# Seven score tiles a pair of heads, of 128 queries, in place of eight of 112, in an attention and feed-forward kernel

## The chip, the cores and the metric

The kernel runs on one core of a Trainium2 chip. The metric is the device time of one execution in microseconds (us). Before the change three runs give a median of 1433.79 us (1432.87 to 1435.07).

## What is computed

Attention over 8 batches and 12 heads, 448 tokens, head size 64, with normed queries and keys, followed by a feed-forward block on 3584 tokens of 768:

```python
q_n, k_n = rmsnorm(q, g_q), rmsnorm(k, g_k)
scores = scale * q_n @ k_n.T
scores = scores - max(scores)            # over the keys, for each query
attn = exp(scores) / (sum + 1e-9)
x = attn @ v                             # heads side by side: 3584 x 768
h = relu(x @ w_in)                       # 768 x 2048
out = (s * h * h + b) @ w_out            # 2048 x 768
```

The change concerns the maximum over the keys alone. It is subtracted before the exponential, and divides out again in `attn`, so it has to be near the true maximum and need not equal it to the last bit.

## The kernel before

**Pairs and slots.** Two heads of a batch make a pair: 48 pairs, 6 for each batch. A pair has 8 slots (`W`), and the outer loop (`for s_ in range(FIRST, NSLOT + LAST + 2)`) walks over 384 slots, with 22 ahead of them and some behind. The order of every engine's instructions, the DMA queue SP among them, is the order in which the program issues them; nothing is reordered by a scheduler. `jobs[s]` is a table of what else each slot issues, filled by `at(slot, function, ...)`; within a slot the jobs stand in the order of the pairs and, for a pair, of the `at` calls. With s0 = 8p the first slot of pair p, the places that matter are:

- s0 - 19 and s0 - 15: `load_kq` and `spread` (DMA in: keys and queries, and the inverse norms, for head 0 and head 1); four slots later `scale` (GpSimd L362, VectorE L363), two more and `split_kq` (ScalarE casts into `ka` and `qa`, L381 and L382, then GpSimd L384 and L385). The first 9 pairs go through `load_rows`, `norm_rows`, `turn` and `split_turned` in place of these (L255 to L291).
- s0 - 10 and s0 - 6: `double_kb`, a DMA of the keys' high parts from `ka` into `kb` (L388 by way of `move`).
- s0 - 10 to s0 - 3: `score` (L400) and `maximum` (L411), one of each in a slot; a slot s works on unit s + 10 (`AHEAD`).
- s0 - 6 and s0 - 2: `shift`, a DMA that writes the negative maxima of a head as row 64 of `qb` (L388 too).
- s0 to s0 + 7: `score_t`, the transposed scores of 128 keys in two matmuls (L438, then L441, which reads row 64 of `qb`), `exponent`, and two slots later `weigh` (L497), the product with the values.

**Scores, twice.** The kernel multiplies queries and keys twice. The transposed product goes on to the exponential. The other (`score`) serves the maxima alone: with queries on the partitions, VectorE can reduce over the 448 keys. Its weights are 112 queries, every fourth one of a head (`"k (p c) -> k c p"`, c of 4); its moving operand is the head's 448 keys; four such tiles for a head, eight for a pair. `maximum` reduces each to one column of `nmx` (112 by 8). The partitions 0 to 63 of `ka` hold the keys' high parts and 64 to 127 the low parts, and both halves of `qa` the queries' high parts.

**Filler.** While batch b's attention runs, TensorE also does the first feed-forward product of batch b - 1 (`ffn_in`, L208): six matmuls in each slot from slot 56 on (`FILL`), 288 a batch. The feed-forward weights are converted from 64-bit words on the way (L133 to L151 for `w_in`, up to slot 90; L156 to L172 for `w_out`). Behind the slots come a short stretch without attention and then the second product (L814).

Of the kernel before, what the change touches and what calls it, by code (L numbers as in the profile page):

```python
# [9 lines left out]
F32 = mybir.dt.float32  # L10
F32R = mybir.dt.float32r
I32 = mybir.dt.int32
AF = mybir.ActivationFunctionType
ALU = mybir.AluOpType
AX = mybir.AxisListType
# [24 lines left out]
STEPS = {0: 4, 1: 5, 5: 6, 6: 7, 9: 8, 10: 9, 12: 10, 13: 11}  # L40

LATE = 12

OUT = (92, *range(110, 141, 6), *(48 * b + i for b in range(3, 8) for i in range(14, 43, 7)))

# [2 lines left out]
def attention_then_relu2_ffn(  # L48
# [30 lines left out]
    V, S, G, T = nc.vector, nc.scalar, nc.gpsimd, nc.tensor  # L79

    NPAIR, P, _, SEQ = kq.shape
# [4 lines left out]
    D = P // 2  # L86
    NP = NPAIR // B
    H = 2 * NP
    TILES = 2 * SEQ // P
    NV = 2 * NP  # L90
    NR = rows0.shape[0]
    NQ = 4
    QC = SEQ // NQ
# [8 lines left out]
    W = 8  # L102
# [137 lines left out]
    lp = last.enter_context(tc.tile_pool(name="lpool", bufs=1, side="right"))  # L240
    ap = early.enter_context(tc.tile_pool(name="apool", bufs=1))
    if True:
        raws, kqs, invs, vrs, nmxs, shs, tks = ({} for _ in range(7))
        sts, movers, avs, uzs, zts, zbs, us = ({} for _ in range(7))

        def load(p):
            raw = raws[p] = ap.tile([P, 2, TILES, D], F32, tag="raw", name=f"raw{p}")
            nc.sync.dma_start(raw, kq_rows[p])
# [8 lines left out]
        def norm_rows(p, j):  # L257
            raw = raws[p, j].rearrange("p t c d -> p (t c) d")
            n = 2 * NQ
            sq = lp.tile([QC, n, D], F32, tag="al", bufs=2, name=f"sq{p}_{j}")  # L260
            S.activation(
                sq.rearrange("p i d -> p (i d)"), raw.rearrange("p i d -> p (i d)"), AF.Square
            )
            yield
            ssq = ap.tile([QC, n], F32, tag="ssq", bufs=2, name=f"ssq{p}_{j}")
            V.tensor_reduce(out=ssq, in_=sq, op=ALU.add, axis=AX.X)
            yield
            ri = ap.tile([QC, n], F32, tag="ri", bufs=2, name=f"ri{p}_{j}")
            G.tensor_scalar(ri, ssq, 1.0 / D, 1e-6, ALU.mult, ALU.add)
            G.tensor_tensor(ri, ri, mhalf[:QC, :n], ALU.pow)  # L270
            G.tensor_tensor(raw, raw, ri.unsqueeze(2).broadcast_to([QC, n, D]), ALU.mult)
# [40 lines left out]
        def load_v(p):  # L312
            if p < NV:
                to = vrs[p] = ap.tile([P, NKC, 3, D], F32, tag=f"vs{p % 2}", name=f"vf{p}")
# [18 lines left out]
        def norm(p):  # L333

            raw = raws.pop(p).rearrange("p t c d -> p (t c) d")
            n = 2 * TILES
            S.activation(
# [10 lines left out]
        def keep(p):  # L348
            nc.sync.dma_start(
                i_d[p].rearrange("t (p c) -> p t c", c=TILES),  # L350
                invs.pop(p).rearrange("p (t c) -> p t c", c=TILES),
            )
# [14 lines left out]
        ka = [ap.tile([P, 2 * SEQ], F32R, name=f"ka{n}") for n in range(2)]  # L367
        qa = [ap.tile([P, 2 * SEQ], F32R, name=f"qa{n}") for n in range(2)]
        kb = [ap.tile([P, 2 * SEQ], F32R, name=f"kb{n}") for n in range(2)]
        qb = [ap.tile([P, 2 * SEQ], F32R, name=f"qb{n}") for n in range(2)]  # L370
        for t in qb:
            G.memset(t[D:P].bitcast(F32), 0.0)
        for t in kb:
            G.memset(t[D:P].bitcast(F32), 0.0)
            G.memset(t[D : D + 1].bitcast(F32), 1.0)

        def split_kq(p, j):

            t, n = kqs.pop((p, j)), p % 2
            a = slice(j * SEQ, (j + 1) * SEQ)  # L380
            S.copy(ka[n][:, a], t[:, 0])  # L381
            S.copy(qa[n][:, a], t[:, 1])  # L382
            yield
            G.tensor_tensor(ka[n][D:, a], t[D:, 0], ka[n][D:, a].bitcast(F32), ALU.subtract)  # L384
            G.tensor_tensor(qb[n][:D, a], t[:D, 1], qa[n][:D, a].bitcast(F32), ALU.subtract)  # L385

        def move(to, of):
            nc.sync.dma_start(to.bitcast(F32), of.bitcast(F32))  # L388
# [5 lines left out]
        def score(i):  # L394

            p, c = divmod(i, W)
            j, c = divmod(c, NQ)
            sh, bank = psum(f"sh{i}")
            a = slice(j * SEQ, (j + 1) * SEQ)
            T.matmul(  # L400
                sh[:QC, :SEQ], qa[p % 2][:, a].rearrange("k (p c) -> k c p", c=NQ)[:, c],
                ka[p % 2][:, a], start=True, stop=True,
            )
            shs[i] = sh, bank

        def maximum(i):
            p, c = divmod(i, W)
            if c == 0:
                nmxs[p] = ap.tile([QC, W], F32R, tag="nmx", bufs=2, name=f"nmx{p}")
            sh, bank = shs.pop(i)  # L410
            V.tensor_reduce(  # L411
                out=nmxs[p][:, c : c + 1], in_=sh[:QC, :SEQ], op=ALU.max, axis=AX.X, negate=True
            )
            free.append(bank)

        def shift(p, part):

            to = qb[p % 2][D : D + 1, part * SEQ : (part + 1) * SEQ]
            move(
                to.rearrange("o (p c) -> o p c", c=NQ), nmxs[p][:, part * NQ : (part + 1) * NQ]  # L420
            )
            if part:
                nmxs.pop(p)

        def chunk(i):
            p, g = divmod(i, W)
            j, kc = divmod(g, NKC)
            return p, j, kc, P if kc < 3 or p < NV else REST

# [17 lines left out]
        def exponent(i):  # L447
            p, j, kc, rows = chunk(i)
            st, bank = sts[i]
            if p < NV:  # L450
                e = lp.tile([P, SEQ], F32, tag="ah", bufs=3, name=f"e{i}")
# [7 lines left out]
        def split_e(i):  # L459
            p, j, kc, rows = chunk(i)  # L460
            if p < NV:
                return
# [4 lines left out]
        def split_e_lo(i):  # L467
            p, j, kc, rows = chunk(i)
            if p < NV:
                return  # L470
# [10 lines left out]
        def weigh(i):  # L481
# [6 lines left out]
            moved = movers.pop(i)  # L488
            if p < NV:
                of = vrs[p].rearrange("p c u d -> p c (u d)")  # L490
# [11 lines left out]
        def take(p, j):  # L502
# [5 lines left out]
            if j == 0:  # L508
                zts[p] = lp.tile([P, TILES], F32, tag="zt", bufs=2, name=f"zt{p}")

        def gather(p, j):
            zt, uz = zts[p], uzs[p, j]
            row = (1 - j) * D
            nc.sync.dma_start(
                zt[j * D : (j + 1) * D], uz[row : row + 1].rearrange("o (p c) -> o p c", c=TILES)
            )
# [6 lines left out]
        def divide(p, step):  # L523

            if step == 1:
                nc.sync.dma_start(z_d[p].rearrange("j (p c) -> (j p) c", c=TILES), zts.pop(p))
            elif step == 2:
                zb = zbs[p] = lp.tile([P, SEQ], F32, tag="zb", name=f"zb{p}")
                for j in range(2):
                    nc.sync.dma_start(  # L530
                        zb[j * D : (j + 1) * D], z_d[p][j : j + 1].broadcast_to([D, SEQ])
                    )
            else:
                zb = zbs.pop(p)
                u = us[p] = lp.tile([P, SEQ], F32, tag="u", bufs=NP, name=f"u{p}")
                for j in range(2):
                    a = slice(j * D, (j + 1) * D)
                    G.tensor_tensor(u[a], uzs.pop((p, j))[a], zb[a], ALU.mult)  # L538
# [96 lines left out]
        def at(s_, f, *a):  # L635
            jobs[s_].append((f, a))

        for p in range(NPAIR):
            s0 = W * p
            if p >= NR:  # L640
                at(s0 - 32, load, p)
                at(s0 - 28, norm, p)
                at(s0 - 24, keep, p)
            for j in range(2):
                s1 = s0 + 4 * j
                if p >= NR:
                    at(s1 - 19, load_kq, p, j)
                    at(s1 - 19, spread, p, j)
                    at(s1 - 15, scale, p, j)
                    at(s1 - 13, split_kq, p, j)  # L650
                else:
                    at(max(s1 - 28, FIRST), load_rows, p, j)
                    at(s1 - 20, norm_rows, p, j)
                    at(s1 - 13, turn, p, j)
                    at(s1 - 12, split_turned, p, j)
                at(s1 - 10, double_kb, p, j)
                at(s1 - 6, shift, p, j)
                at(s1 + 6, take, p, j)
                at(s1 + 7, gather, p, j)
            at(s0 - (9 if p >= NV else 5), load_v, p)  # L660
            if p >= NV:
                at(s0 - 3, split_v, p)
            at(s0 + 13, invert, p)
            at(s0 + 14, divide, p, 1)
            at(s0 + 16, divide, p, 2)
            at(s0 + 18, divide, p, 3)
# [82 lines left out]
        def t_step(k):  # L749
# [3 lines left out]
            if k + 1 < KS:  # L753
                t_sums(k + 1, G if k + 1 < LATE + 2 else V)

# [122 lines left out]
        with tc.manual_schedule(engines=ORDERED):  # L878
            begun = []
            for s_ in range(FIRST, NSLOT + LAST + 2):  # L880
# [5 lines left out]
                if s_ >= NSLOT + 2:  # L886
                    k, of = divmod(s_ - NSLOT - 5, 3)
# [77 lines left out]
            for x in range(ROUNDS):  # L965
                if LATE <= LATE + x < KS:
                    t_step(LATE + x)
                g_load(x + 5)
                g_sums(x + 3)
                g_split(x + 2)  # L970
                p, m = divmod(x, NM)
# [53 lines left out]
```

## Time and profile before

| | |
|---|---|
| median of three runs | 1433.79 us |
| the profiled execution | 1435.51 us, with a span of 1433.0 us and a mean granted TensorE clock of 0.99 |
| TensorE busy | 1394.2 us, 97% of the span |
| VectorE, ScalarE, GpSimd busy | 73%, 60%, 72% |
| score matmuls for maxima (L400) | 384 |
| maxima (L411) | 384, 618 ns each, 236.5 us of VectorE |
| DMA | 237.94 MB, 55.8% of the 16 engines' time |

In the profile PE is TensorE's matmul row and PEld its weight loads, DVE is VectorE, ACT is ScalarE, POOL is GpSimd, and SPq is the queue that issues DMAs. A group of instructions is listed by line, engine, tile written and tiles read, shapes and count; behind the bar stand its busy time, the mean of one in ns, and the idle time of the engine ahead of it with what ended it. The chain of waits follows the last instruction back, at each step to what released it. Matmuls overlap in the record: one that shows 367 ns is followed by the next after about 204 ns.

### The profile page before, as it was taken

How to read it: one execution, taken by the hardware profiler on the slowest of the kernel's cores; microseconds unless marked ns; L12 is line 12 of the kernel's file. 1: busy time of each engine (PE TensorE's matmuls, PEld its weight loads, DVE VectorE, ACT ScalarE, POOL GpSimd, SP SyncE). 2: the span in 40 equal slices, each digit the busy share in tenths (PEclk: the TensorE clock that was granted, in tenths of full speed). 3: DMA queues.
4: the chain of work that ended last, by engine and by line, in shares of the span. 5: the costliest groups of instructions: out<-in, count | busy, mean ns of one | idle time of the engine just before them, and what ended most of it. 6: DMA issues, size and time to landing. Idle time of an engine off the chain costs nothing.

```text
span 1433.0 us, 22188 instructions
## 1 busy us (share of the span) xinstructions
PE 1394.2 (97%) x6996; PEld 1268.3 (89%) x6996; DVE 1048.4 (73%) x1594; ACT 867.0 (60%) x1649; POOL 1031.6 (72%) x941
## 2 busy tenths in 40 slices
PE   7988999999999999999999999989899999999999
PEld 5666778899899899999989989969799999999998
DVE  6998987888888788788788787463666666666665
ACT  4777555777767776777677777543445444444443
POOL 7778888877777777777778776273686776667764
PEclk8999999999999999999999999989999999999999
DMA  4456777777677677677777766243333333333331
GB/s 131 133 153 167 223 230 219 214 225 222 203 235 220 200 233 222 186 235 230 203 211 234 214 179 201 90 140 119 104 104 89 118 96 96 96 102 108 95 95 66
DMA packets 209252, 237.94 MB, mean 166 GB/s; under 512 B 72848, under 2 KB 187024, under 8 KB 209136
## 3 DMA queue, kind: packets, MB, share of 16 engines
q1 hardware_dynamic: 209136, 236.54, 55.8%
q8 instruction: 55, 0.90, 0.3%
q14 instruction: 61, 0.50, 0.1%
HBM read 178.00 MB, written 47.11 MB: 157 GB/s over the span
## 4 chain that ended last, share of the span: by engine, by line
PE 84%; DVE 7%; DMA 3%; POOL 2%; issue 2%; ACT 2%; SPq 0%; DVEq 0%; ACTq 0%; POOLq 0%
PE ph L208 29%; PE m L814 27%; PE av L497 13%; PE sh L400 5%; PE st L438 5%; PE st L441 5%; DMA w64i<-in_dram 1%; DVE nmx L411 1%; DVE wai L140 1%; DVE wai L137 1%; DVE wai L142 1%; POOL u L538 1%; PE tk L278 1%; DVE t L742 1%; DVE wai L145 0%
## 5 line engine op out<-in xcount | busy, mean ns | idle before, releaser
L208 PE MATMUL ph<-x,wih 128*128 128x448 f32 x1536 | 494.6, 368 | 7.1 <-ACT x L545 3.8
L814 PE MATMUL m<-t,gh 128*128 128x384 f32 x1568 | 400.8, 336 | 3.3 <-ACT gh L795 2.6
L208 PEld LDWEIGHTS ph<-x,wih 128*128 128x128 f32 x1536 | 289.8, 189 | 40.7 <-issue 7.8
L208 PE MATMUL ph<-x,wil 128*128 128x448 f32 x768 | 297.1, 387 | 0.0
L411 DVE TENSOR_REDUCE nmx<-sh 112x1 fp32r<-112x448 f32 x384 | 236.5, 618 | 78.1 <-PE sh L400 75.9
L814 PEld LDWEIGHTS m<-t,gh 128*128 128x128 f32 x1568 | 284.0, 188 | 5.4 <-ACT gh L795 3.3
L814 PE MATMUL m<-t,gl 128*128 128x384 f32 x784 | 263.6, 336 | 2.1 <-DVE gl L796 2.1
L457 ACT ACTIVATE st<-st 128x448 f32<-128x448 f32 (+1 forms) x288 | 151.3, 525 | 186.8 <-PE st L441 183.8
L796 DVE TENSOR_TENSOR gl<-g,gh 128x896 fp32r<-128x896 f32 x112 | 130.0, 1161 | 145.4 <-ACT gh L795 141.4
L795 ACT CAST gh<-g 128x896 fp32r<-128x896 f32 x112 | 105.8, 945 | 215.4 <-POOL g L785 157.2
L781 POOL TENSOR_TENSOR g<-g 128x256 f32<-128x256 f32 x112 | 97.2, 868 | 133.0 <-DVE g L780 133.0
L497 PE MATMUL av<-ah,vs 128*128 128x448 f32 x576 | 165.0, 367 | 0.8 <-DVE al L478 0.5
L400 PE MATMUL sh<-ka,qa 128*112 128x448 f32 x384 | 148.3, 388 | 16.5 <-DVE ka L290 8.4
L208 PEld LDWEIGHTS ph<-x,wil 128*128 128x128 f32 x768 | 144.9, 189 | 19.3 <-issue 7.9
L438 PE MATMUL st<-qa,ka 128*128 128x448 f32 (+1 forms) x384 | 158.1, 412 | 2.4 <-ACT e L453 1.7
L465 ACT CAST ah<-st 128x448 fp32r<-128x448 f32 (+1 forms) x288 | 153.6, 533 | 1.3
L814 PEld LDWEIGHTS m<-t,gl 128*128 128x128 f32 x784 | 147.6, 188 | 3.4 <-DVE gl L796 3.4
L538 POOL TENSOR_TENSOR u<-uz,zb 64x448 f32<-64x448 f32 x96 | 133.2, 1387 | 20.3 <-DMA zb<-z_d 16.1
L478 DVE TENSOR_TENSOR al<-st,ah 128x448 fp32r<-128x448 f32 x216 | 132.7, 614 | 18.7 <-ACT ah L465 15.8
L441 PE MATMUL st<-qb,kb 128*128 128x448 f32 (+1 forms) x384 | 140.6, 366 | 0.0
L384 POOL TENSOR_TENSOR ka<-kq,ka 64x448 fp32r<-64x448 f32 x78 | 97.5, 1250 | 52.2 <-ACT ka L381 48.9
L400 PEld LDWEIGHTS sh<-ka,qa 128*112 128x112 f32 x384 | 107.5, 281 | 30.0 <-ACT wih L148 5.4
(85 smaller groups left out, 2432.6 us busy)
## 6 DMA issues: line engine op xcount, KB each, us to landing
kq<-in_dram SPq DMA_DIRECT2D x78, 448.0 KB, 5.0
rb<-i_d SPq DMA_DIRECT2D x78, 448.0 KB, 5.8
r_d<-r SPq DMA_DIRECT2D x128, 224.0 KB, 3.1
raw<-in_dram SPq DMA_DIRECT2D x39, 448.0 KB, 5.0
raw<-r_d SPq DMA_DIRECT2D x64, 256.0 KB, 2.8
w64i<-in_dram SPq DMA_DIRECT2D x24, 512.0 KB, 4.7
w64o<-in_dram SPq DMA_DIRECT2D x32, 384.0 KB, 5.1
kb<-ka SPq DMA_DIRECT2D x96, 112.0 KB, 3.6
```

What stands on the lines that cost most here:

```text
L208: T.matmul(ph[:, :SEQ], w[:, cc, f0 : f0 + P], xs[b, cc][:, part, :], start=n == 0, stop=n == 3 * NCC - 1,)
L400: T.matmul(sh[:QC, :SEQ], qa[p % 2][:, a].rearrange("k (p c) -> k c p", c=NQ)[:, c], ka[p % 2][:, a], start=True, stop=True,)
L411: V.tensor_reduce(out=nmxs[p][:, c : c + 1], in_=sh[:QC, :SEQ], op=ALU.max, axis=AX.X, negate=True)
L438: T.matmul(st[:rows, :SEQ], ka[n][:, keys], qa[n][:, q], start=True, stop=False)
L441: T.matmul(st[:rows, :SEQ], kb[n][:, keys], qb[n][:, q], start=False, stop=True,)
L457: S.activation(st[:rows, :SEQ], st[:rows, :SEQ], AF.Exp)
L465: S.copy(ah[:rows], sts[i][0][:rows, :SEQ])
L478: V.tensor_tensor(al, st[:rows, :SEQ], ah[:rows].bitcast(F32), ALU.subtract)
L497: T.matmul(av[:, :SEQ], x, a, start=kc == 0 and m == 0, stop=kc == 3 and m == len(todo) - 1,)
L538: G.tensor_tensor(u[a], uzs.pop((p, j))[a], zb[a], ALU.mult)
L796: V.tensor_tensor(gl, g9[:, 1:8], gh.bitcast(F32), ALU.subtract)
L814: T.matmul(to, g[:, sa], w, start=m == 0 and n == 0, stop=m == NM - 1 and n == 2,)
```

## The change

Each head's first 384 queries go through three score tiles of 128 queries (every third one). The last 64 queries of both heads share one tile. For it two tiles are new: `both_k`, with the high parts of head 0's keys on partitions 0 to 63 and of head 1's on 64 to 127, filled by two DMAs a pair (`stack_k`); and `both_q`, zero but for two 64 by 64 blocks on the diagonal, filled by two ScalarE copies a pair (`stack_q`). So this tile's scores leave out the keys' low parts. The slot table `UNITS` keeps units 0, 1, 2 for head 0, 4, 5, 7 for head 1 and 6 for the shared tile; the fourth slot of each eight has no score and no maximum. The maxima of the shared tile are moved into `qb` by two more DMAs (`shift_rest`).

The space is made by two moves: the squares of `norm_rows` (`sq`) go from a tag with two buffers to the tag `vr` with one, and the results `u` have five buffers and not six, with the last pair's in a buffer of `al`.

```diff
+UNITS = {0: (0, 0), 1: (0, 1), 2: (0, 2), 4: (1, 0), 5: (1, 1), 6: (2, 0), 7: (1, 2)}
...
+    NF = SEQ // P
+    FULL = NF * P
...
-            sq = lp.tile([QC, n, D], F32, tag="al", bufs=2, name=f"sq{p}_{j}")
+            sq = ap.tile([QC, n, D], F32, tag="vr", name=f"sq{p}_{j}")
...
+        both_k = ap.tile([P, SEQ], F32R, name="both_k")
+        both_q = ap.tile([P, P], F32R, name="both_q")
+        G.memset(both_q.bitcast(F32), 0.0)
+
+        def stack_k(p, j):
+            move(both_k[j * D : (j + 1) * D], ka[p % 2][:D, j * SEQ : (j + 1) * SEQ])
+
+        def stack_q(p):
+            for j in range(2):
+                a = slice(j * D, (j + 1) * D)
+                S.copy(both_q[a, a], qa[p % 2][a, j * SEQ + FULL : (j + 1) * SEQ])
...
-            j, c = divmod(c, NQ)
+            if c not in UNITS:
+                return
+            j, c = UNITS[c]
             sh, bank = psum(f"sh{i}")
-            T.matmul(
-                sh[:QC, :SEQ], qa[p % 2][:, a].rearrange("k (p c) -> k c p", c=NQ)[:, c],
-                ka[p % 2][:, a], start=True, stop=True,
-            )
+            if j < 2:
+                T.matmul(
+                    sh[:, :SEQ],
+                    qa[p % 2][:, a][:, :FULL].rearrange("k (p c) -> k c p", c=NF)[:, c],
+                    ka[p % 2][:, a], start=True, stop=True,
+                )
+            else:
+                T.matmul(sh[:, :SEQ], both_q, both_k, start=True, stop=True)
...
-                out=nmxs[p][:, c : c + 1], in_=sh[:QC, :SEQ], op=ALU.max, axis=AX.X, negate=True
+                out=nmxs[p][:, u : u + 1], in_=sh[:, :SEQ], op=ALU.max, axis=AX.X, negate=True
...
+        def shift_rest(p, part):
+            to = qb[p % 2][D : D + 1, part * SEQ + FULL : (part + 1) * SEQ]
+            move(to.rearrange("o (p c) -> o p c", c=1), nmxs[p][part * D : (part + 1) * D, 2 * NF :])
...
+                of = dict(tag="al", bufs=2) if p == NPAIR - 1 else dict(tag="u", bufs=NP - 1)
...
+            at(s0 - 10, stack_k, p, 0)
+            at(s0 - 7, stack_k, p, 1)
+            at(s0 - 7, stack_q, p)
+            for j in range(2):
+                at(s0 - 3, shift_rest, p, j)
```

More of the change, by code (lines that the diff above doesn't have):

```diff
@@ L396, in score @@
             p, c = divmod(i, W)
-            j, c = divmod(c, NQ)
+            if c not in UNITS:
+                return
+            j, c = UNITS[c]
             sh, bank = psum(f"sh{i}")
-            a = slice(j * SEQ, (j + 1) * SEQ)
-            T.matmul(
-                sh[:QC, :SEQ], qa[p % 2][:, a].rearrange("k (p c) -> k c p", c=NQ)[:, c],
-                ka[p % 2][:, a], start=True, stop=True,
-            )
+            if j < 2:
+                a = slice(j * SEQ, (j + 1) * SEQ)
+                T.matmul(
[5 more added lines that the diff above has]
+                T.matmul(sh[:, :SEQ], both_q, both_k, start=True, stop=True)
             shs[i] = sh, bank
@@ L408, in maximum @@
             if c == 0:
-                nmxs[p] = ap.tile([QC, W], F32R, tag="nmx", bufs=2, name=f"nmx{p}")
+                nmxs[p] = ap.tile([P, 2 * NF + 1], F32R, tag="nmx", bufs=2, name=f"nmx{p}")
+            if c not in UNITS:
+                return
+            j, c = UNITS[c]
             sh, bank = shs.pop(i)
+            u = j * NF + c
             V.tensor_reduce(
-                out=nmxs[p][:, c : c + 1], in_=sh[:QC, :SEQ], op=ALU.max, axis=AX.X, negate=True
+                out=nmxs[p][:, u : u + 1], in_=sh[:, :SEQ], op=ALU.max, axis=AX.X, negate=True
             )
@@ L416, in shift @@
         def shift(p, part):
-            to = qb[p % 2][D : D + 1, part * SEQ : (part + 1) * SEQ]
+            nmx, row = nmxs[p], qb[p % 2][D : D + 1, part * SEQ : (part + 1) * SEQ]
             move(
-                to.rearrange("o (p c) -> o p c", c=NQ), nmxs[p][:, part * NQ : (part + 1) * NQ]
-            )
-            if part:
-                nmxs.pop(p)
+                row[:, :FULL].rearrange("o (p c) -> o p c", c=NF),
+                nmx[:, part * NF : (part + 1) * NF],
+            )
+        def shift_rest(p, part):
+            to = qb[p % 2][D : D + 1, part * SEQ + FULL : (part + 1) * SEQ]
+            move(to.rearrange("o (p c) -> o p c", c=1), nmxs[p][part * D : (part + 1) * D, 2 * NF :])
         def chunk(i):
@@ L534, in divide @@
                 zb = zbs.pop(p)
-                u = us[p] = lp.tile([P, SEQ], F32, tag="u", bufs=NP, name=f"u{p}")
+                of = dict(tag="al", bufs=2) if p == NPAIR - 1 else dict(tag="u", bufs=NP - 1)
+                u = us[p] = lp.tile([P, SEQ], F32, name=f"u{p}", **of)
                 for j in range(2):
```

## The prediction

> **What bounds the kernel now.** I read the page first, for the engines and the chain of waits.
>
> ```profile
> PE 1394.2 (97%) x6996; PEld 1268.3 (89%) x6996; DVE 1048.4 (73%) x1594; ACT 867.0 (60%) x1649; POOL 1031.6 (72%) x941
> PE 84%; DVE 7%; DMA 3%; POOL 2%; issue 2%; ACT 2%; SPq 0%; DVEq 0%; ACTq 0%; POOLq 0%
> PE ph L208 29%; PE m L814 27%; PE av L497 13%; PE sh L400 5%; PE st L438 5%; PE st L441 5%; DMA w64i<-in_dram 1%; DVE nmx L411 1%; DVE wai L140 1%; DVE wai L137 1%; DVE wai L142 1%; POOL u L538 1%; PE tk L278 1%; DVE t L742 1%; DVE wai L145 0%
> ```
>
> TensorE carries 84% of the chain, and the score matmul itself (L400) 5%; the maximum (L411) only 1%. An average over stages hides where that is so. The busy times by stretch come next (PE, PEld, DVE, ACT, POOL, clock, DMA share, GB/s):
>
> ```profile
> 40.00:60.00 20.00, 17.59 (x76) 12.28 (x74) 18.49 (x30) 14.69 (x30) 12.96 (x13) 1.00 0.41 113
> 100.00:120.00 20.00, 17.72 (x73) 11.88 (x71) 18.62 (x32) 16.53 (x32) 17.59 (x16) 1.00 0.51 142
> 140.00:180.00 40.00, 38.89 (x163) 30.67 (x162) 37.10 (x47) 22.60 (x44) 35.62 (x28) 1.00 0.75 231
> 262.00:377.00 115.00, 115.00 (x564) 105.24 (x564) 94.96 (x156) 83.22 (x173) 89.67 (x67) 1.00 0.74 222
> ```
>
> There are two regimes. From 262 us on TensorE is never idle, 115.00 of 115 us, and 564 matmuls share that time: 204 ns each. That is one batch of 48 slots exactly (48 times 2 transposed scores, 1 score and 6 of filler, and 132 products with the values). Here a matmul less is time less. Early, no engine is full: VectorE leads with 18.5 of 20 us, TensorE follows with 17.6, and the chain passes between them. So I take the chain of waits by stage, in four windows (0 to 30, 30 to 130, 130 to 240, 240 to 900 us):
>
> ```profile
> by line: DMA w64i<-in_dram 21.4%; PE tk L278 10.0%; DVE nmx L411 7.6%; DVE wai L137 7.4%; PE sh L400 7.2%; issue 5.5%; DVE wai L145 4.7%; DVE wai L140 4.7%; DVE wai L142 4.3%; ACT wih L148 4.2%; ACT qa L287 3.5%; ACT ka L286 3.1%; SPq L255
> ...
> by line: PE av L497 13.2%; issue 10.0%; PE sh L400 7.3%; DVE nmx L411 5.9%; PE tk L278 5.4%; DMA raw<-in_dram 5.0%; DVE wai L140 4.8%; PE st L438 4.2%; POOL ri L270 3.9%; DVE wai L142 3.8%; PE st L441 3.7%; ACT qa L288 3.4%; DVE ka L290 3.1
> ...
> by line: PE ph L208 16.1%; DMA w64i<-in_dram 11.7%; PE av L497 10.6%; issue 7.0%; DVE wai L140 6.5%; DVE wai L137 6.3%; DVE nmx L411 5.3%; DMA zt<-uz 5.1%; DVE wai L142 4.9%; POOL u L538 4.5%; DVE ssq L342 3.7%; PE sh L400 3.6%; DVE kq L363
> ...
> by line: PE ph L208 49.7%; PE av L497 23.6%; PE st L438 8.4%; PE st L441 8.4%; PE sh L400 8.3%; DMA zb<-z_d 0.4%; DVE kq L363 0.2%; DVE ssq L342 0.2%; issue 0.1%; DVE ah L478 0.1%; DVE nmx L411 0.1%; ACT qa L382 0.1%; ACT st L457 0.1%; DVE
> ```
>
> In the last window the score is 8.3% of the chain and the maximum 0.1%; before 240 us both stand on it at 4 to 8%.
>
> **What is taken away.** One score and one maximum of eight go, in each of 48 pairs. I price them as an eighth of what the two hold of the chain, since a path that stays is a floor for the new time:
>
> - 0 to 30 us: (7.6 + 7.2)% of 30, by 8: 0.6 us.
> - 30 to 130: (5.9 + 7.3)% of 100, by 8: 1.6 us.
> - 130 to 240: (5.3 + 3.6)% of 110, by 8: 1.2 us.
> - 240 to 900: (0.1 + 8.3)% of 660, by 8: 6.9 us.
>
> That is 10.3 us. The last term agrees with a count: at 115 us for six pairs 660 us hold 34 of them, times 204 ns, 7.0 us. The other three are soft. If VectorE were the only bound, each of the first 8 pairs would give a whole maximum, and so would the 4 after them. The groups, with shapes kept apart:
>
> ```profile
> L411 DVE TENSOR_REDUCE nmx<-sh 112x1 fp32r<-112x448 f32 x384 | 236.5, 618 | 78.1 <-PE sh L400 75.9
> L400 PEld LDWEIGHTS sh<-ka,qa 128*112 128x112 f32 x384 | 107.5, 281 | 30.0 <-ACT wih L148 5.4 <-ACT qa L288 3.6 <-ACT e L453 3.3
> L441 PEld LDWEIGHTS st<-qb,kb 128*128 128x128 f32 x312 | 59.1, 190 | 12.9 <-issue 8.7
> L381 ACT CAST ka<-kq 128x448 fp32r<-128x448 f32 x78 | 43.2, 554 | 0.0
> L739 ACT CAST t<-w 128x192 fp32r<-128x192 f32 x16 | 5.6, 349 | 0.6 <-POOL w L731 0.4
> ```
>
> 12 times 0.618 (the first row) is 7.4 us in place of 3.4, so the upper end is 14.3 us. If those stages give nothing, because GpSimd (17.6 of 20 us at 100) or the DMAs hold them, it is 6.9 us.
>
> **The wider tile.** The reduction and the matmul run over the same 448 columns; 128 partitions for 112 add nothing to either. What widens is the weight load. Its row shows 281 ns for 112 strided columns, against 190 for 128 that lie together: longer than the 204 ns step. Does it show? The timeline in the full stage (start, duration):
>
> ```profile
> 402.72 0.37 PE L208 MATMUL ph<-x,wih 128*128 128x448 f32 x1
> ...
> 402.92 0.36 PE L208 MATMUL ph<-x,wil 128*128 128x448 f32 x1
> 402.93 0.28 PEld L400 LDWEIGHTS sh<-ka,qa 128*112 128x112 f32 x1
> 403.13 0.37 PE L400 MATMUL sh<-ka,qa 128*112 128x448 f32 x1
> ...
> 403.33 0.57 PE L208 MATMUL ph<-x,wih 128*128 128x448 f32 x2
> ```
>
> The starts are 0.20, 0.21 and 0.20 apart: the load of 281 ns costs 0.01 us at most. By columns it grows to 281 times 128/112, 321 ns. I take zero, and keep 40 ns for 6 of 7 units (288 in all, 11.5 us) as the other end, in a rival. The Trainium skill (TensorE: Matmul & The Clock Gate, Back-to-back issue gap) says that weight load and matmul together set the spacing in a stream of pairs, and its section on LDWEIGHTS that a load goes with the number of columns, at 1.2 a ns. By that rule 16 columns more would be 13 ns a unit, 3.8 us for 288 and a sum of some 5 us in place of mine; the trace does not follow the figure, since 112 columns take longer than 128 here, and the step does not show the load.
>
> **What is added.** Two ScalarE copies of 64 columns a pair. The two CAST rows differ by 256 columns and 205 ns, so 64 columns come to about 0.25 us (an estimate; 0.20 to 0.35 as bounds): 0.5 us a pair. In the full stage ScalarE is at 83 of 115 us and six pairs add 3.0; it stays under TensorE, and slot s0 - 7, where the copies stand, has no score to serve. Early, a quarter of 8 times 0.5 is my guess of what reaches the chain: 1.0 us, between 0 and 4.
>
> Four DMAs a pair: two like `kb<-ka` and two like `qb<-nmx`, from the DMA view of 262 to 377 us (KB each, median us from issue to landing):
>
> ```profile
> q1 hardware_dynamic: 19933, 25.40, 74.0%
> ...
> rb<-i_d SPq DMA_DIRECT2D x12, 448.0 KB, 5.8
> ...
> kb<-ka SPq DMA_DIRECT2D x12, 112.0 KB, 4.0
> ...
> qb<-nmx SPq DMA_DIRECT2D x12, 1.8 KB, 4.4
> ```
>
> 25.40 MB for six pairs is 4.2 MB a pair; 0.23 MB more is 5%, and takes the share from 0.74 to 0.78. Nothing waits for bandwidth there. At 130 to 240 us the chain does hold DMAs (11.7 and 5.1% of 110, 18.5 us); 5% of that is 0.9 us, between 0 and 2.
>
> **The new waits.** `shift_rest` at s0 - 3 waits on SP for the shared tile's maximum, issued a slot before; behind it on SP are the next-but-one pair's keys and norms, and the one who waits for it is L441 in slot s0, three slots on. Pair 20, with s0 at 392.7 us:
>
> ```profile
> 384.01 0.37 PE L400 MATMUL sh<-ka,qa 128*112 128x448 f32 x1
> 385.09 0.60 SPq L298 DMA_DIRECT2D kq<-in_dram  x1
> 385.74 0.59 SPq L358 DMA_DIRECT2D rb<-i_d  x1
> 385.80 0.62 DVE L411 TENSOR_REDUCE nmx<-sh 112x1 fp32r<-112x448 f32 x1
> ...
> 392.95 0.37 PE L441 MATMUL st<-qb,kb 128*128 128x448 f32 x1
> ...
> 395.02 1.57 DVE L363 SCALAR_TENSOR_TENSOR kq<-kq,gqk,rb 128x448 f32<-128x448 f32 x1
> ```
>
> The maximum ends at 386.42. With the 4.4 us of `qb<-nmx` the rest lands at 390.8 and L441 starts at 392.95: 2.1 us spare. The loads behind it move from 385.09 to about 387.7 (two issues of some 0.6 us), so `rb` is issued near 388.3 and lands at 394.1 by its 5.8 us; L363 reads it at 395.02: 0.9 us spare. Both waits cost nothing, and both margins are thin. The early slots are shorter, and there the same two margins are, for pair 1 (the shared unit's maximum and the L441 that needs it; the keys that `stack_k` moves and the shared score):
>
> ```profile
> 29.36 0.51 ACT L286 CAST ka<-tk 64x448 fp32r<-64x448 f32 x1
> ...
> 34.89 0.37 PE L400 MATMUL sh<-ka,qa 128*112 128x448 f32 x1
> ...
> 36.27 0.62 DVE L411 TENSOR_REDUCE nmx<-sh 112x1 fp32r<-112x448 f32 x1
> ...
> 41.48 0.37 PE L441 MATMUL st<-qb,kb 128*128 128x448 f32 x1
> ```
>
> 36.89 + 4.4 is 41.3, just ahead of 41.48; 29.87 + 4.0 is 33.9, ahead of 34.89. The DMA share is 0.41 there, so landings should be quicker. `sq` in one buffer costs nothing while VectorE's sum, a slot later, ends before the next square four slots on; without that cover it is one wait of a 0.6 us square, 18 times at most, early. The buffers of `u` are freed by `split_x` ahead of their next use by four slots at least, and the last pair's has a buffer of `al` that is no longer in use.
>
> **Sum.** 10.3 - 1.0 - 0.9 = 8.4 us. The profiled execution would go from 1435.51 to 1427.1; it lies 1.7 us above the median, and the median goes from 1433.79 to 1425.4. What follows the attention is not touched and moves ahead as a whole.
>
> **Rivals.**
>
> *The early stages give nothing* (GpSimd at 17.6 of 20 us, weights arriving by DMA). For: the 18.5 us of DMA on the chain. Against: VectorE is the fullest engine there. 6.9 us less 1.9 of costs: 1428.8.
>
> *L441 waits for the rest of the maxima.* Slower. It decides from a landing of 6.5 us after the maximum (392.95 less 386.42), or from a VectorE that runs that much later. `rb` takes 5.8 us at the median, so 7 or 7.5 us behind a full queue are not far; each half microsecond beyond the point stalls TensorE for it in 34 pairs: 17 us, less my 8.4, 1442. Against: the shift is now ahead of `kq` and `rb` in the queue, not behind them, and should land sooner than 4.4 us.
>
> *The strided weight load surfaces.* Price 11.5 us against 8.4: 1436.9. It decides where a load is longer than the matmuls ahead of it can cover. Against: the step of 0.20 at 281 ns.
>
> *The change doesn't do what it says*: a slot without a score keeps its length, because another engine paces slots. Then nothing moves, 1433.8. Against: TensorE idle for 0.00 us in the full stage.
>
> **Chances.** Forecast 0.68, early stages empty 0.15, waiting L441 0.07, weight load 0.05, no effect 0.05. A measurement of this kernel can tell about 0.2% from no change, 2.9 us. The first two are beyond that: with a part of the rest, faster 0.84; slower 0.09, same 0.07. The range goes from 1420.0 (the upper end of 14.3 us, nearly) to 1430.0, under the empty early stages with the higher costs.
>
> **What would show it.** Right: L400 and L411 336 times each; 558 matmuls a batch in about 113.9 us at a PE still full; a step of 0.20 us around L400 with its load near 320 ns; L411 still 618 ns. Wrong: idle time of L441 or its load after a DMA `qb<-nmx`, of L400 after `both_k`, of L363 after `rb`; a batch of 115 us; a first 240 us no shorter than before.

## The result, and the profile after

The changed kernel takes 1452.93 us (median of four runs, 1450.06 to 1457.93) beside 1433.67 us for the kernel before on the same chip: a ratio of 1.0138, 95% interval 1.0123 to 1.0153. It is 19.3 us slower; the prediction had 8.4 us faster, and the time lies far outside its range. The profiled run is the slowest of the four, 1457.93 us with a span of 1456.2.

The page after, its engines, the DMA queue, and the chain of waits by engine and by line:

```profile
PE 1392.9 (96%) x6948; PEld 1262.9 (87%) x6948; DVE 1047.2 (72%) x1546; ACT 892.9 (61%) x1745; POOL 1002.2 (69%) x942
...
q1 hardware_dynamic: 226032, 247.56, 58.6%
...
PE 73%; DMA 10%; DVE 6%; issue 3%; ACT 3%; POOL 3%; SPq 2%; POOLq 0%; DVEq 0%; ACTq 0%
PE m L849 27%; PE ph L212 23%; PE av L526 11%; PE st L467 4%; PE st L470 4%; PE sh L419 3%; DMA both_k<-ka 2%; DMA w64i<-in_dram 2%; DMA z_d<-zt 1%; DVE nmx L437 1%; DMA zb<-z_d 1%; PE tk L282 1%; PE sh L425 1%; DMA raw<-in_dram 1%; DMA qb<-nmx 1%
```

48 matmuls and 48 VectorE operations have gone, as the change says. But TensorE has lost 11 points of the chain, and DMAs have gone from 3 to 10%. Among them is a transfer that did not exist before, `both_k<-ka`. The full stage, by a window (us, then busy us of PE, PEld, DVE, ACT and POOL, the clock, the DMA share and GB/s) and by three of the five longest pieces of the chain between 262 and 900 us (start, length):

```profile
262.00:377.00 115.00, 112.33 (x549) 102.00 (x548) 93.99 (x149) 84.86 (x182) 84.02 (x68) 1.00 0.77 228
```

```profile
528.58 6.10 DMA both_k<-ka
646.77 6.32 DMA both_k<-ka
764.65 6.82 DMA both_k<-ka
```

TensorE was busy for 115.00 of 115 us; now it stands still for 2.7 of them, and 549 matmuls fit where 558 would make the new batch. The three pieces lie 118 us apart, which is one batch with its stands: the same place in each batch. One such stand from near by, by SP's queue and TensorE around 416 us (the shared score of pair 21; start, duration):

```profile
407.99 2.19 SPq L559 DMA_DIRECT2D zb<-z_d  x2
410.28 0.54 SPq L353 DMA_DIRECT2D i_d<-ri  x1
410.87 0.46 SPq L252 DMA_DIRECT2D raw<-in_dram  x1
411.38 0.42 SPq L160 DMA_DIRECT2D w64o<-in_dram  x1
411.90 0.48 SPq L404 DMA_DIRECT2D both_k<-ka  x1
```

```profile
416.35 0.36 PE L212 MATMUL ph<-x,wih 128*128 128x448 f32 x1
416.55 0.36 PE L212 MATMUL ph<-x,wil 128*128 128x448 f32 x1
418.66 0.44 PE L425 MATMUL sh<-both_k,both_q 128*128 128x448 f32 x1 [1.75 <-issue]
```

The second `stack_k` is issued at 411.90, behind five other issues of its slots; it lands at 418.6; the shared score (L425) starts at 418.66, 2.1 us after its neighbour and not 0.2. The transfers of one full stage batch say part of why (KB each, median us from issue to landing):

```profile
kb<-ka SPq DMA_DIRECT2D x12, 112.0 KB, 5.2
both_k<-ka SPq DMA_DIRECT2D x12, 112.0 KB, 4.9
```

The same `kb<-ka` took 4.0 before. The row for `both_k` mixes both transfers of a pair. The second one alone, counted over pairs 12 to 44, lands 5.3 us after its issue at the median and 6.8 at most. From its issue to the place of the shared score there are 6.5 us at the median, but only 3.6 at the least, because SP issues it up to 4.1 us after the first matmul of its slot. So 1.2 us are spare at the median, and 28 of these 33 pairs do not stand. Five do (16, 21, 27, 33 and 39), where both ends come together: the issue is 3.6 to 5.7 us ahead of the score, and the landing takes 5.6 to 6.8. Over the run twelve shared scores stand still for `both_k`, 21.8 us together (the steps of TensorE above the usual ones, counted in the trace), 9.4 of them in the first eight pairs, the first for pair 1 at 36.59 us. After the longest of them, 4.02 us before 115.29, TensorE also runs at half its clock (PE, PEld, DVE, ACT, POOL, clock, DMA share, GB/s):

```profile
114.00:121.00 7.00, 5.71 (x11) 3.83 (x12) 4.31 (x8) 2.35 (x5) 5.24 (x8) 0.52 0.43 104
```

Half clock is granted here for 6.8 us, for another 6.8 us from 216.7 us on, in a stand of 3.0 us, and for 3.4 us after a stand of 2.82 us at 653. The Trainium skill (TensorE: Matmul & The Clock Gate, Part 1: The HAM clock gate) has the gate decide by windows of about 3.4 us; these stretches are two, two and one of them long.

### The profile page after: what moved, and what is told of

It reads as the page before. It is cut to its first block, busy times and chain, and to the rows that moved or that the text cites. A ratio compares the mean times of both kernels' runs of the same rounds, so it can differ in the third digit from the quotient of the medians.

```text
span 1456.2 us, 22597 instructions
## 1 busy us (share of the span) xinstructions
PE 1392.9 (96%) x6948; PEld 1262.9 (87%) x6948; DVE 1047.2 (72%) x1546; ACT 892.9 (61%) x1745; POOL 1002.2 (69%) x942
## 4 chain that ended last, share of the span: by engine, by line
PE 73%; DMA 10%; DVE 6%; issue 3%; ACT 3%; POOL 3%; SPq 2%; POOLq 0%; DVEq 0%; ACTq 0%
PE m L849 27%; PE ph L212 23%; PE av L526 11%; PE st L467 4%; PE st L470 4%; PE sh L419 3%; DMA both_k<-ka 2%; DMA w64i<-in_dram 2%; DMA z_d<-zt 1%; DVE nmx L437 1%; DMA zb<-z_d 1%; PE tk L282 1%; PE sh L425 1%; DMA raw<-in_dram 1%; DMA qb<-nmx 1%
## 5 line engine op out<-in xcount | busy, mean ns | idle before, releaser
L437 DVE TENSOR_REDUCE nmx<-sh 128x1 fp32r<-128x448 f32 x336 | 207.3, 618 | 82.0 <-PE sh L419 47.2
L816 POOL TENSOR_TENSOR g<-g 128x256 f32<-128x256 f32 x112 | 95.8, 856 | 132.4 <-DVE g L815 132.4
L526 PE MATMUL av<-ah,vs 128*128 128x448 f32 x576 | 164.9, 367 | 2.9 <-DVE ah L507 1.8
L568 POOL TENSOR_TENSOR u<-uz,zb 64x448 f32<-64x448 f32 x96 | 119.0, 1239 | 50.5 <-DMA zb<-z_d 46.9
L470 PE MATMUL st<-qb,kb 128*128 128x448 f32 (+1 forms) x384 | 141.3, 368 | 0.0
L419 PE MATMUL sh<-ka,qa 128*128 128x448 f32 x288 | 111.9, 389 | 15.5 <-DVE ka L294 8.1
L820 POOL TENSOR_TENSOR g<-g 128x256 f32<-128x256 f32 x112 | 121.0, 1080 | 0.0
```

The costliest lines, as they stand in the source:

```text
L419: T.matmul(sh[:, :SEQ], qa[p % 2][:, a][:, :FULL].rearrange("k (p c) -> k c p", c=NF)[:, c], ka[p % 2][:, a], start=True, stop=True,)
L437: V.tensor_reduce(out=nmxs[p][:, u : u + 1], in_=sh[:, :SEQ], op=ALU.max, axis=AX.X, negate=True)
L470: T.matmul(st[:rows, :SEQ], kb[n][:, keys], qb[n][:, q], start=False, stop=True,)
L526: T.matmul(av[:, :SEQ], x, a, start=kc == 0 and m == 0, stop=kc == 3 and m == len(todo) - 1,)
L820: G.tensor_tensor(g9[:, 5:7], g9[:, 0:9:8], g9[:, 1:8:6], ALU.subtract)
```

## The experiments

Each edit is to the changed kernel if nothing else is said. A ratio is to the kernel before, measured beside each run (medians of 1433.1 to 1433.9 us), with its 95% interval in brackets.

**Is it the wait for `both_k`?** The theory: it alone makes the change slower, and without it the predicted gain is there. The rivals: the copies, the traffic, or SP held by `shift_rest`. First, the second `stack_k` is issued a slot or two sooner (e1), or ScalarE copies the keys in place of the DMAs (e2):

```diff
-            at(s0 - 7, stack_k, p, 1)
+            at(s0 - (9 if p >= NR else 8), stack_k, p, 1)     # e1
-            move(both_k[...], ka[...])
+            S.copy(both_k[...], ka[...])                      # e2
```

> One edit to the changed kernel: the DMA that stacks head 1's keys is issued two slots earlier (one for the first 9 pairs). Theory A: the loss is the landing of both_k, since the shared score L425 stands still for some 22 us in all, 12 of them from pair 9 on and 9 before. By A the later 12 us go and about half of the earlier ones: about 1437 us, and no L425 wait on both_k after 170 us. Theory B, the added DMA traffic and SP issues as such: the same 192 DMAs are issued, so less than 3 us is won, 1450 or more. Theory C, the queue SP held up by the wait of shift_rest for a maximum: unchanged too, 1450 or more.

Measured: 1434.39 us (1430.39 to 1438.01), ratio 1.0003 (0.999 to 1.0015): 18.5 us less than the changed kernel; one stand of 0.72 us is left, and no half clock between 24 and 944 us. With the earlier issue the landing itself falls to 2.6 us at the median (pairs 12 to 44).

> One edit to the changed kernel: both_k is filled by two ScalarE copies of 64 by 448 a pair, at the same places, in place of two DMAs. Theory A: all 22 us of standing still at L425 go, and the stalls behind VectorE (some 10 us, two slots a batch, at L526) stay: about 1431 us. Theory B: the traffic goes as well, and with it both kinds of stall: 1421. Theory C: the 10 us stay as long as shift_rest stands where it is: 1431. If ScalarE, with 1.0 us a pair more, becomes the bound: over 1435, with L425 or the exponentials waiting for ScalarE.

Measured: 1436.46 us, ratio 1.0020 (1.0009 to 1.0031). From 240 to 905 us TensorE waits for VectorE's `al` (8.3 us in all), and not for ScalarE. And the other way, a slot later in all pairs:

```diff
-            at(s0 - 7, stack_k, p, 1)
+            at(s0 - 6, stack_k, p, 1)
```

> The changed kernel with the second of the two DMAs into both_k issued one slot later still (s0 - 6 in place of s0 - 7), nothing else. The wait for both_k: the shared score (L425) is not moved, so it stands still for that DMA in nearly every pair and not in 12 of 48, by up to a slot more (2.0 to 2.4 us) less what stands ahead of it on SP in the new slot: 1 to 2.4 us in each of 48 pairs on top of 1452.9, 1500 to 1560 us. If both_k is only the last named of several that are late together (ScalarE's both_q, VectorE), a later DMA adds little: 1453 to 1470.

Measured: 1537.6 us, 85 us more; the stands for `both_k` sum to some 87 us in its trace, beside 22. The wait is what makes the change slower, and its size follows the place of the DMA. But with the wait gone the kernel is level with the one before: some nine microseconds of predicted gain are missing (1434.4 beside a forecast of 1425.4). That became the question.

**Is it the order of the early slots, or SP behind `shift_rest`?** e3 has the shared tile first among the units of the second half and `shift_rest` sooner; e4 spreads the copies; f2 (on e1) leaves the first and not the fourth slot free:

```diff
-UNITS = {..., 4: (1, 0), 5: (1, 1), 6: (2, 0), 7: (1, 2)}
+UNITS = {..., 4: (2, 0), 5: (1, 0), 6: (1, 1), 7: (1, 2)}     # e3, on e2
-                at(s0 - 3, shift_rest, p, j)
+                at(s0 - 5, shift_rest, p, j)                  # e3
+UNITS = {..., 4: (1, 0), 5: (2, 0), 6: (1, 1), 7: (1, 2)}     # e4, on e2; first stack_k s0 - 8, stack_q s0 - 6, shift_rest s0 - 4
+UNITS = {1: (0, 0), 2: (0, 1), 3: (0, 2), 4: (1, 0), 5: (1, 1), 6: (2, 0), 7: (1, 2)}   # f2, on e1
```

> The same ScalarE copies, and the shared tile scored two slots earlier (first of the second half), with shift_rest at s0 - 5 in place of s0 - 3, so that SP no longer waits for a maximum just ahead of the keys and norms of a later pair. Theory C: the 10 us of stalls behind VectorE go, beyond the keys by ScalarE alone: about 1421. Theories A and B: no difference from the keys by ScalarE alone, within 2 us.

Measured: 1448.8 us. New stands of 2.1 to 2.9 us in the early pairs, for ScalarE's `both_q`, with five stretches of 3.4 us at half clock behind them; the full stage as in e2.

> The same ScalarE copies, spread over the slots s0 - 8, s0 - 7 and s0 - 6, the shared tile scored one slot earlier than in the changed kernel and shift_rest at s0 - 4. If ScalarE's copies delay exponentials, spreading them wins 1 to 3 us over the run with the shared tile first; else the two agree within 1 us. Theory C: about 1421, as shift_rest again no longer stands just ahead of the loads.

Measured: 1437.15 us.

> The kernel with the keys stacked early, and one more edit: the slot without a score is the first of the eight (head 0's three tiles move one slot on) and not the fourth. Theory F: in the first 130 us the free fourth slot gains nothing, since the next slot's score waits for VectorE's ka all the same; with the first slot free, the score that waits for ka at a head's start has one slot more, and the waits of 1 to 2 us there go: 3 to 6 us by 130 us, nothing later, about 1430. Rival: the early stage is held by VectorE's sum of work: under 1 us.

Measured: 1435.69 us; pair 12 starts at 238.7 us, no sooner than in e1 (237.4) or before (238.2). None of these orders brings the gain back.

**Is it VectorE's subtractions at a batch's end?** In e1 the products (L526) wait for VectorE at a batch's end; the six subtractions of `split_x` stand in six slots there. They are spread on e1 (f1), with f2 as well (f3), in the kernel before (f4), and on e1 without batch 0 (g4):

```diff
-            at(end(b + 1) - (2 if b < B - 1 else 4) + g, split_x, b, g)
+            at(end(b + 1) + ((-5, -4, -2, -1, 2, 3)[g] if b < B - 1 else g - 4), split_x, b, g)
```

> The kernel with the keys stacked early, and one more edit: the six splits of x at a batch's end (ScalarE L575, VectorE L576) stand in the slots -5, -4, -2, -1, +2 and +3 about the batch's end, not in six slots in a row from -2. Theory D: in the full stage the gain of 1.2 us a batch is given back there, because two of these subtractions in a row run 1.6 us each beside GpSimd, where the kernel before had 0.6 us ones between, and the products L526 then wait for VectorE (1 to 1.6 us a batch). By D those waits go and a batch falls from 114.8 to 113.6 us: 5 to 7 us less than with the keys early alone, about 1428. Rival E, late loads of rb hold VectorE: no difference.

Measured: 1436.42 us.

> Both edits together on top of the keys stacked early. If D and F hold they act in different stages and add: about 1424, 9 to 10 us under the kernel before. If the shortened early stage or the moved splits collide elsewhere: no better than the better of the two.

Measured: 1435.38 us.

> Control: the kernel before with only the splits of x spread in the same way. TensorE stands still nowhere at a batch's end in that kernel, so by D nothing is won: 1433 to 1434. If it is won here too (3 us or more), the spread is a gain of its own that has nothing to do with the scores.

Measured: 1436.27 us, slower than the kernel before by 0.2%: spreading them has a price of its own, a stand of some 5 us in batch 0 (4.4 in f1).

> The kernel with the keys moved earlier, and the six subtractions at a batch's end spread over nine slots for the batches 1 to 6, batch 0 as before. If the products' wait for VectorE at a batch's end takes the full stage's gain: 0.7 us a batch back without the stand that the spread of batch 0's cost, 1430 to 1431.5 where the keys alone give 1434.4. If the spread itself costs (new waits of the filler on x), 1434 to 1437 as with batch 0 spread too.

Measured: 1433.77 us. The products' wait for VectorE is hardly smaller (4.2 us in eleven waits from 240 to 905 us, where e1 has 5.3 in thirteen), a batch takes 114.77 us beside 114.83, and the gain stays missing.

**Is the gain there at all?** g3 is the kernel before with one score and one maximum of eight left out and nothing put in; g2 is the changed kernel with nothing stacked.

```diff
+            if c == 3:
+                return                                        # g3: in score and maximum of the kernel before
-            at(s0 - 10, stack_k, p, 0)
-            at(s0 - 7, stack_k, p, 1)
-            at(s0 - 7, stack_q, p)                            # g2
```

> The kernel before with the fourth score and the fourth maximum of each eight left out and nothing put in: no wider tile, no new DMA, no copy. It leaves out the maxima of a quarter of each first head's queries (a constant, 660, stands for them). The prediction's price of what is taken away is 10.3 us: 1423.5. If the free slot is taken up by VectorE's other work (waits of the products at a batch's end, keys that come no sooner in the early slots), 2 to 5 us: 1429 to 1432, with a batch of 48 slots near 114.8 us and not 114.1, and pair 12 starting at 237 us or later and not at 234.8.

Measured: 1425.46 us (1423.4 to 1427.33), ratio 0.9945 (0.9933 to 0.9958).

> The changed kernel without stack_k and stack_q: both_k and both_q hold constants, so the two DMAs and the two ScalarE copies a pair and their waits are gone, while the shared score, its maximum and its two DMAs into qb stay. It leaves out the true maxima of the last 64 queries of each head (a constant, 660, stands for them). If traffic and copies eat the gain of seven units in place of eight, it comes back here: 1423.5 to 1426. If the gain itself is mostly not there, because VectorE and the order of its work take up the free slot, it stays near the kernel with the keys moved earlier: 1431 to 1435.

Measured: 1436.71 us, ratio 1.002 (1.001 to 1.003). So the gain exists, 7.7 us; and neither the DMAs into `both_k` nor the copies eat it, since it is missing without them too. The waits of TensorE from 240 to 905 us, of g3 and then of g2 (us in total, times, longest):

```profile
PE av L505 <- ACT x L553: 1.3, 5, 0.3
PE av L505 <- DVE al L486: 0.5, 1, 0.5
PE av L505 <- DVE ah L486: 0.5, 1, 0.5
```

```profile
PE av L527 <- DVE al L508: 7.1, 7, 1.5
PE av L527 <- ACT x L576: 1.3, 5, 0.3
PE av L527 <- DVE ah L508: 0.5, 1, 0.5
```

Both have as many matmuls and as many operations on VectorE, but in g2 VectorE is late at every batch's end. One of the things that differ is the maximum: 112 partitions in g3, 128 in g2.

**The maximum's partitions.** The theory, called the port theory in the expectations, is that the number of partitions of a maximum decides whether VectorE or GpSimd goes first behind it. The runs show who goes first, not what in the chip the two engines share. To try it, a pair of kernels differ in nothing else. In both, the queries of the kernel before lie in 512 columns a head (the last 64 zero), so that its eight score tiles are 128 wide; i5 reduces 112 partitions, i3 all 128:

```diff
-                out=nmxs[p][:QC, c : c + 1], in_=sh[:QC, :SEQ], op=ALU.max, axis=AX.X, negate=True   # i5
+                out=nmxs[p][:, c : c + 1], in_=sh[:, :SEQ], op=ALU.max, axis=AX.X, negate=True       # i3
```

> The kernel before with eight scores a pair as before, but each matmul and each weight load 128 queries wide (the queries of a head lie in 512 columns, 64 of them zero), and the maximum still over 112 partitions. If it is the maximum over 128 partitions that hands VectorE's time to GpSimd (the port theory), this is the kernel before: 1433 to 1434, with GpSimd operations that start in a maximum and meet VectorE's kq near 2.09 us and kq at 0.68 us. If the wider score matmul or its load costs, 1437 to 1441.

> The same, with the maximum over all 128 partitions (16 of them serve nothing), and no other difference. Port theory: GpSimd operations that start in a maximum now go through at 1.15 us and the kq behind the maximum takes 1.43 us in place of 0.68, as in the changed kernel; products wait for VectorE at each batch's end; 4 to 9 us more than with 112 partitions, 1437 to 1442. If the partitions of the maximum don't matter and the kernels differ for another reason (the shifts' DMAs, addresses): within 1.5 us of its neighbour, 1432 to 1435.

Measured: i5 1441.73 us (1440.06 to 1442.62), i3 1453.45 us (1452.26 to 1454.49): 11.7 us for sixteen idle partitions more in each of 384 maxima, beyond the 4 to 9 expected. (That i5 itself lies some 8 us above the kernel before is its weight load, below.) VectorE and GpSimd at the end of a batch, in i5 (start, duration):

```profile
378.27 0.62 DVE L416 TENSOR_REDUCE nmx<-sh 112x1 fp32r<-112x448 f32 x1
378.81 0.68 DVE L364 SCALAR_TENSOR_TENSOR kq<-kq,gqk,rb 128x448 f32<-128x448 f32 x1
379.40 0.62 DVE L552 TENSOR_TENSOR x<-u,x 128x448 fp32r<-128x448 f32 x1
```

```profile
378.58 3.68 POOL L544 TENSOR_TENSOR u<-uz,zb 64x448 f32<-64x448 f32 x2
```

and the same operations in i3:

```profile
381.26 0.62 DVE L416 TENSOR_REDUCE nmx<-sh 128x1 fp32r<-128x448 f32 x1
381.80 1.39 DVE L364 SCALAR_TENSOR_TENSOR kq<-kq,gqk,rb 128x448 f32<-128x448 f32 x1
383.11 1.56 DVE L552 TENSOR_TENSOR x<-u,x 128x448 fp32r<-128x448 f32 x1
```

```profile
381.57 2.63 POOL L544 TENSOR_TENSOR u<-uz,zb 64x448 f32<-64x448 f32 x2
```

In both, GpSimd's `u` starts 0.31 us into a maximum and 0.23 us ahead of VectorE's `kq`. Behind the maximum of 112 partitions VectorE goes first: `kq` and `x` take 0.68 and 0.62 us, and GpSimd's two operations 3.68 together. Behind the one of 128 GpSimd goes first: its two take 2.63, and `kq` and `x` 1.39 and 1.56. VectorE has lost 1.65 us just where the products wait for it, as TensorE's waits from 240 to 905 us show, of i5 and of i3:

```profile
PE av L503 <- DVE al L484: 0.5, 1, 0.5
```

```profile
PE av L503 <- DVE al L484: 10.2, 7, 1.7
```

10.2 less 0.5 is 9.7 of the 11.7 us. Counted over pairs 12 to 45 of each trace, for GpSimd operations that start during a maximum and still run when `kq`, next on VectorE, starts (means):

| kernel | partitions of the maximum | times | GpSimd's operation, us | `kq`, us |
|---|---|---|---|---|
| before | 112 | 18 | 2.09 | 0.68 |
| g3 | 112 | 15 | 2.14 | 0.68 |
| i1 | 112 | 12 | 1.94 | 0.68 |
| after | 128 | 14 | 1.15 | 1.43 |
| e1 | 128 | 12 | 1.15 | 1.48 |
| i3 | 128 | 19 | 1.15 | 1.41 |
| i4 | 127 | 15 | 1.15 | 1.46 |

In i5 fourteen of 18 went like its rows above, and four as in i3 (1.15 and 1.26 us). Those four are the only ones with 112 partitions in which GpSimd started as early as 0.11 to 0.12 us into the maximum; in the fourteen, and in all of before, g3 and i1, it started 0.2 us or more into it. In i3 all 19 went one way, the four that started as early too. So the partitions decide for a start from about 0.2 us into the maximum on; what lies between 0.12 and 0.2 us no run shows.

In the changed kernel the same step is i1 (e1 with the maximum over 112 partitions), with 127 in i4, and the rival that the place of the output decides in i2 (e1 with `nmx` 8 columns wide, as before):

```diff
-                out=nmxs[p][:, u : u + 1], in_=sh[:, :SEQ], op=ALU.max, axis=AX.X, negate=True
+                out=nmxs[p][:112, u : u + 1], in_=sh[:112, :SEQ], op=ALU.max, axis=AX.X, negate=True   # i1; 127 in i4
-                nmxs[p] = ap.tile([P, 2 * NF + 1], ...)
+                nmxs[p] = ap.tile([P, W], ...)                                                         # i2
```

> The changed kernel with the keys moved earlier and the maximum taken over 112 of the 128 partitions; the scores, the DMAs and the copies stay. It leaves out the maxima of 16 queries of each tile (a constant, 660, stands for them). Port theory: kq behind a maximum back at 0.68 us, no wait of the products at a batch's end, 34 pairs in 644 us and not 648: 1426 to 1430, where the keys moved earlier alone gave 1434.4. Without it: 1433 to 1436.

Measured: 1426.91 us (1425.45 to 1429.26), ratio 0.9951 (0.9939 to 0.9963), where e1 gave 1434.39; the batch from pair 18 on takes 114.11 us beside 114.83 in e1 and 114.14 in g3.

> The changed kernel with the keys moved earlier and the tile of the maxima 8 columns wide, as in the kernel before, and not 7; the maximum stays over 128 partitions. If it is the place of the maximum's output and not its partitions that decides who goes first: as with 112 partitions, 1426 to 1430. Port theory by partitions: as the keys moved earlier alone, 1433 to 1436.

Measured: 1435.54 us, ratio 1.001 (0.9999 to 1.0021). The width of `nmx` does nothing that can be told.

> As the changed kernel with the keys moved earlier and the maximum over 112 partitions, but over 127. It leaves out the maximum of one query of each tile (a constant, 660, stands for it). If the full 128 partitions are what is special: 1426 to 1428, with kq behind a maximum at 0.68 us. If the point lies between 112 and 127: 1433 to 1436, with kq near 1.4 us.

Measured: 1434.37 us, ratio 1.0012 (0.9998 to 1.0025). 127 partitions act like 128; the point lies between 112 and 127 and was not searched, since seven tiles need 128. What in the chip draws it these runs do not show. (In i1 and i4 the maxima lie in two fixed tiles; i4 has them too and gains nothing, so it is not they.) The kept traces show less of the step from e1 to i1 than the medians do: e1's is of its fastest run, 1430.39 us, and i1's of its slowest, 1429.26 us.

**The sum.** Leaving out a unit: -7.7 (g3). What i1 has beyond it, the DMAs, the copies and the wider scores: 1.5 (1426.91 less 1425.46). The maximum over 128 partitions: 7.5 (e1 less i1). The wait for `both_k`, with the half clock behind it: 18.5 (after less e1). Together +19.8, beside the 19.3 measured. The steps lead from kernel to kernel, so their sum has to come out; it gives the size of each and is no proof. The 1.5 is the least certain: the runs of i1 and g3 overlap, and g2, without the stacking, is 2.3 us slower than e1 and not faster. No kernel with all maxima in it beats the kernel before by what can be told; e1 and g4 come nearest, at 1.0003 and 1.0004 (0.9994 to 1.0015 for g4).

## Why the prediction was wrong, step by step

**The new waits: the step that failed first.** The prediction looked at the wait for `both_k` in one early pair, with a median landing of 4.0 us of another transfer in another stage, from the moment ScalarE's cast ends ("29.87 + 4.0 is 33.9, ahead of 34.89"), and called it free ("Both waits cost nothing"). Three things were left out. The DMA does not start when its keys are ready but when SP comes to it: in pair 1 of the changed kernel the cast ends at 29.73 us, SP issues the transfer at 32.90, and it lands at 36.50. The landing of 3.6 us was no worse than assumed; the 3.2 us ahead of it were put at nothing, and pair 1, the example itself, stood for 1.90 us. The full stage was not worked out at all for this wait, though it has 36 of 48 pairs; there 1.2 us are spare at the median, and five pairs stand. And the end of the landings was not taken (5.6 to 6.8 us in those five), as its own rival did for another wait. The step cost 18.5 us.

**The wider tile: the other failed step.** "128 partitions for 112 add nothing to either" is true of the maximum's own time, 618 ns before and after. It is not true of what comes behind it: 7.5 us, by way of who goes first behind it, VectorE or GpSimd. No row of the profile before showed a maximum over 128 partitions. By the prediction's own method its cost had to be bounded from both sides, and it was set to zero. The group of its neighbour `kq` shows it, from 262 to 900 us, before and after (878 and 1106 ns each; 893, 920 and 921 in g3, i5 and i1, and 1065 to 1111 in e1, g2, i3 and i4):

```profile
L363 DVE SCALAR_TENSOR_TENSOR kq<-kq,gqk,rb 128x448 f32<-128x448 f32 x66 | 57.9, 878 | 1.9 <-DMA rb<-i_d 1.9
L367 DVE SCALAR_TENSOR_TENSOR kq<-kq,gqk,rb 128x448 f32<-128x448 f32 x66 | 73.0, 1106 | 4.2 <-DMA qb<-nmx 2.6 <-DMA rb<-i_d 0.7 <-issue 0.5
```

**What is taken away.** The eighth of the chain was right where TensorE is the bound: from pair 12 to pair 46 the profiles take 650.2 us before and 643.9 in g3, 6.3 less for a forecast of 6.9. Before pair 12 they gain 1.9 (238.2 to 236.3) for a forecast of 3.4: little more than half of the soft terms came. In all 7.7 for 10.3.

**The weight load.** No cost, as forecast, but for another reason. The load did not grow to 321 ns; it fell, as a batch of the changed kernel and then of i5 shows:

```profile
L419 PEld LDWEIGHTS sh<-ka,qa 128*128 128x128 f32 x36 | 9.0, 251 | 0.6
```

```profile
L404 PEld LDWEIGHTS sh<-ka,qa 128*128 128x128 f32 x47 | 14.5, 309 | 0.8
```

The columns of the change are every third query, those of i5 every fourth as in the kernel before. At 251 ns the step stays at 0.20 us, as it did at 281; at 309 the load shows, in i5's matmuls:

```profile
401.71 0.37 PE L208 MATMUL ph<-x,wil 128*128 128x448 f32 x1
401.92 0.39 PE L404 MATMUL sh<-ka,qa 128*128 128x448 f32 x1
402.15 0.56 PE L208 MATMUL ph<-x,wih 128*128 128x448 f32 x2
```

0.23 us behind the score in place of 0.20, and i5 takes some 8 us more than the kernel before (ratio 1.0053, 1.0041 to 1.0065); 27 ns in each of the 288 scores of 36 pairs is 7.8 us. So the rival's mechanism is real, at a load just above the one that was seen to be hidden; the smaller stride spared the change from it.

**What held.** L470 does not wait for the rest of the maxima in the full stage; the shift of 0.2 KB lands in 2.6 us at the median. The costs of copies and traffic, 1.9 us forecast, came to about 1.5, as uncertain as that figure is. `sq` and `u` were not tried alone. The rival on the slow side had the right mechanism, a landing of up to some 7 us behind a full queue, at the wrong wait.

## What to carry to other kernels

Work out each new wait at its tightest stage, from the time at which the queue reaches the issue, and with the slow end of the landings and the late end of the issues, not the medians: here 1.2 us to spare at the median did not keep five pairs from standing. Where the ends do not fit, issue the transfer a slot sooner before anything is measured. When a change alters the shape of an operation, look at its neighbours and not only at its own duration: VectorE and GpSimd take time from each other in ways that the mean of the altered operation's own group does not show. And when a forecast gain fails to appear, run the gain alone first (leave the work out, put nothing in): it tells at once whether it was never there or is given back.

## What the runs showed that was not expected

- A GpSimd operation that starts 0.2 us or more into a maximum waits for VectorE's next operations when the maximum is over 112 partitions (1.9 to 2.1 us as means), and takes its turn first when it is over 127 or 128 (1.15 us), at the price of 0.7 to 0.8 us for VectorE's next one. The Trainium skill (SBUF — State Buffer, SBUF: two separate sides) says that of a GpSimd operation and a VectorE one with two SBUF inputs, as `kq` is, the one that starts first gets the shared port pair for the whole instruction. By the recorded starts GpSimd was first in i5 and i3 alike, 0.23 us ahead of `kq`; i3 follows the rule, i5 does not.
- Some kernels with the wide maximum spread more from run to run: 1430.39 to 1439.79 in twelve runs of i4, 1430.39 to 1438.01 in ten of e1, beside 1425.45 to 1429.26 in six of i1. i3 has the wide maximum too, and its four runs lie within 2.3 us. What makes the others spread is not shown.
- A strided weight load goes by the stride too: 281 ns for 112 columns at every fourth, 309 for 128 at every fourth, 251 for 128 at every third.
